# A transformer block on one core: DMA transposes, aligned padded layouts, and MLP blocks paired to 256 tokens

## The chip, the cores and the metric

The kernel runs on one core of one Trainium2 chip. Times are device microseconds (us) of one execution. The metric is the median over several executions. A run counts as "fast" if it is within 1.5% of the fastest run of the same kernel in its batch.

## The reference

One block of a transformer in bf16: S = 2048 tokens, D = 448, 16 heads of 28, MLP width F = 1792. A conditioning vector gives six rows (shift, scale and gate for each half).

```python
mod = (silu(c) @ w_mod)             # six rows: sa, ca, ga, sb, cb, gb
h = layernorm(x) * (1 + ca) + sa
x = x + ga * A(h)                   # attention: 8 keys per query, every second token
h = layernorm(x) * (1 + cb) + sb
x = x + gb * B(h)                   # B: y = layernorm(h); gelu(y @ w1 + b1) @ w2 + b2
return x
```

Because a query sees every second token only, the kernel splits the tokens into two streams of 1024, and a query then sees 8 neighbours of its stream.

## The kernel before

The matmuls of this kernel hold the contracted features on partitions in both operands, while its layernorms leave tokens on partitions, so the kernel transposes the activations in between. This happens twice for each 128-token block: `z` before q/k/v, and `y` before the first MLP matmul. Before the change TensorE does it by multiplying with an identity, four 128x128 pieces into PSUM, and VectorE copies the result to SBUF:

```python
def transpose_tiles(dst_ps, col_slice, src, nrows_src, koff):
    for kt in range(KT):
        nc.tensor.transpose(out=dst_ps[:, kt, col_slice], in_=src[0:nrows_src, koff[kt]:koff[kt] + 128],
                            identity=ident[0:nrows_src, 0:nrows_src])

def front_end_ln(c4):                       # z of four blocks
    ...
    for pair in range(2):
        ptr = ps_small([128, KT, 256], BF16, "ptr")
        ...
            normalize(z[:, 0:D], x_all[:, bs4[i], :], mv, rs, i)
            transpose_tiles(ptr, slice(bi * 128, (bi + 1) * 128), z, 128, KOFF_A)
        nc.vector.tensor_copy(out=hT[:, :, col0:col0 + 256], in_=ptr[:])

def mlp_front(b):                           # y of one block, first MLP matmul, gelu
    pty = ps_small([128, KT, 128], BF16, "pty")
    ...                                     # two layernorms on VectorE, with a pow on GpSimd in each
    normalize(yb[:, 0:D], h2[:], mv2, rs2, 0)
    transpose_tiles(pty, slice(0, 128), yb, 128, KOFF_A)
    nc.vector.tensor_copy(out=yT[:], in_=pty[:])
    for fq in range(0, FT, 8):
        ...     # w1: 128x128 weights, 128 columns of yT; p1 is shared with the logits
        g = nc.scalar.activation(out=hm[:, fq:fq + nf, :], in_=p1[:, 0:nf, :], func=ACT.Gelu_apprx_tanh)

def mlp_back(b, hm):                        # second MLP matmul, residual, store
    for ft in range(FT):
        nc.tensor.matmul(p2[:], lhsT=hm[:, ft, :], rhs=w2_s[:, ft, :], ...)
```

The kernel alternates between groups of attention blocks (exp on ScalarE) and groups of MLP blocks (gelu on ScalarE), so that ScalarE changes its table seldom (the trace has ten table loads of 1.28 us each: five at the gelu, four at the attention's exp, one in the setup). The second MLP matmul of a group is held back and handed out to the attention blocks that follow, one MLP block to each, as filler for TensorE:

```python
phases = [(range(0, 5), [0, 1]), (range(5, 9), [2, 3, 4, 5]), (range(9, 14), [6, 7, 8, 9]),
          (range(14, 16), [10, 11, 12]), (range(16, 18), [13, 14, 15])]
for (gs, mlp_bs) in phases:
    for g in gs:
        attention_block(...)
        if pending_back: mlp_back(*pending_back.pop(0))     # one filler per attention block
        if g in fe_after: front_end_ln(fe_after[g]); front_end_qk(fe_after[g])
    ...
    for b in mlp_bs: mlp_front(b); pending_back.append((b, hm))
```

The order of instructions within each engine's queue is chosen by a scheduler from the data dependencies; the timelines below show the order in which they ran.

The softmax here doesn't subtract the row's maximum and nothing guards it: scores larger than these inputs give would overflow.

## Time and profile before

The median of the first four runs is 267.75 us (266.85 to 269.57). The profiled run is the slowest of these, 269.57 us with a span of 267.6 us.

The busy table and the slices of the profile of the kernel before. A digit is the busy share of one fortieth of the span in tenths; PEclk is the clock that TensorE was granted, in tenths of full speed.

```profile
...
PE 210.6 (79%) x2216; PEld 142.6 (53%) x2220; DVE 157.6 (59%) x360; ACT 103.0 (39%) x136; POOL 69.4 (26%) x107
...
PE   0004895984987797999896999999899889995995
...
PEclk9999997998699999999997999999999999999799
...
```

The groups that the change touches (line, engine, operation, out and in, count; then busy time in us and mean ns of one; then idle time of the engine just before them and what ended it):

```profile
...
L381 PE MATMUL p<-yT,w_s 128*128 128x128 bf16 x896 | 56.0, 225 | 5.7 <-DVE yT L372 5.4 <-ACT hm L385 0.3
...
L372 DVE COPY yT<-pty 128x512 bf16<-128x512 bf16 x16 | 6.5, 415 | 1.5 <-PE pty L165 1.5
...
L165 PE MATMUL ptr<-ident,zbuf 128*128 128x128 bf16 x64 | 6.2, 241 | 24.0 <-DVE zbuf L160 23.6 <-DVE gbb_bc L287 0.3
L165 PE MATMUL pty<-ident,ybuf 128*128 128x128 bf16 x64 | 5.7, 219 | 4.9 <-DVE ybuf L160 2.5 <-DVE ob L396 1.9 <-DVE kT L197 0.5
L183 DVE COPY hT<-ptr 128x1024 bf16<-128x1024 bf16 x8 | 5.3, 677 | 0.1
...
```

The transposes cost 11.9 us of TensorE and their copies 11.8 us of VectorE. That is the busy time that a DMA transpose takes off the two busiest engines.

What TensorE waited for (us in total, number of waits, longest):

```profile
...
PE p L381 <- DVE yT L372: 5.4, 3, 2.7
PE pq L191 <- DVE kT L197: 5.2, 2, 3.7
PE pb_ga L268 <- DMA wmod<-in_w_mod_dram: 2.8, 1, 2.8
PE pty L165 <- DVE ybuf L160: 2.5, 1, 2.5
...
PE pty L165 <- DVE ob L396: 1.9, 1, 1.9
...
```

And the round trip of `y` in the timeline (start, length, engine, instruction, count). Before the matmul at 105.10 there are two transposes on TensorE and one copy on VectorE:

```profile
...
103.87 0.38 PE L165 MATMUL pty<-ident,ybuf 128*128 128x128 bf16 x4
...
104.03 0.68 DVE L197 CAST kT<-pq 128x512 bf16<-128x512 f32 x1
104.63 0.41 DVE L372 COPY yT<-pty 128x512 bf16<-128x512 bf16 x1
104.77 0.38 PE L165 MATMUL pty<-ident,ybuf 128*128 128x128 bf16 x4 [0.52 <-DVE kT L197]
...
105.10 3.29 PE L381 MATMUL p<-yT,w_s 128*128 128x128 bf16 x56
...
```

### The profile page before, as it was taken

What the parts mean: (1) busy time and instruction counts of PE and PEld (TensorE: products, weight loads), DVE (VectorE), ACT (ScalarE), POOL (GpSimd) and SP (SyncE); (2) the same over time, 40 slices, a digit from 0 to 9 for tenths busy, and PEclk for the clock granted to TensorE, in tenths of its full rate; (3) what the DMA queues carried; (4) which work ended last, traced back from release to release, by engine and by line L of the source; (5) the groups of instructions that cost most, each with busy time, mean ns of one, the idle gap of its engine ahead of it and who ended that gap; (6) DMA issues with size and microseconds to landing.
All of it is one profiled execution on the core that took longest, in us unless ns stands there. A gap on an engine that the chain in (4) does not pass through costs nothing.

```text
span 267.6 us, 5246 instructions
## 1 busy us (share of the span) xinstructions
PE 210.6 (79%) x2216; PEld 142.6 (53%) x2220; DVE 157.6 (59%) x360; ACT 103.0 (39%) x136; POOL 69.4 (26%) x107
## 2 busy tenths in 40 slices
PE   0004895984987797999896999999899889995995
PEld 0003332641553555756775866578855488554962
DVE  0199981898386888046888065797526740576101
ACT  0200230870142240874651754455473236722220
POOL 5066150399013132002342001333101300023000
PEclk9999997998699999999997999999999999999799
DMA  7997344000000000000000000000000100000001
GB/s 235 237 327 209 126 114 147 0 2 0 0 0 2 0 0 2 4 17 21 0 2 0 2 20 17 17 20 2 2 0 20 36 20 2 17 17 20 2 16 35
DMA packets 9544, 11.45 MB, mean 43 GB/s; under 512 B 1265, under 2 KB 7729, under 8 KB 9522
## 3 DMA queue, kind: packets, MB, share of 16 engines
q1 hardware_dynamic: 6610, 7.81, 9.7%
q10 hardware_dynamic: 2912, 3.33, 4.0%
q8 instruction: 17, 0.28, 0.4%
q14 instruction: 5, 0.04, 0.1%
HBM read 9.29 MB, written 1.84 MB: 42 GB/s over the span
## 4 chain that ended last, share of the span: by engine, by line
PE 38%; DVE 33%; POOL 9%; DMA 7%; issue 6%; ACT 5%; SPq 1%; POOLq 0%; ACTq 0%
PE p L381 13%; PE p L393 9%; DVE st_ln L151 6%; POOL rs_ln L156 5%; PE po L335 5%; DVE et L330 4%; DMA x_all<-in_A_x_dram 3%; DMA wmod<-in_w_mod_dram 3%; PE pv L309 3%; DVE on L339 2%; DVE ob L396 2%; DVE h L364 2%; ACT et L326 2%; DVE x_all L352 2%; DVE z L160 2%
## 5 line engine op out<-in xcount | busy, mean ns | idle before, releaser
L381 PE MATMUL p<-yT,w_s 128*128 128x128 bf16 x896 | 56.0, 225 | 5.7 <-DVE yT L372 5.4
L381 PEld LDWEIGHTS <-w_s 128*128 128x128 bf16 x896 | 53.9, 101 | 7.4 <-DVE yT L372 4.1
L393 PE MATMUL p<-w_s,hm 128*128 128x448 bf16 x224 | 47.2, 353 | 0.3 <-ACT vbuf L311 0.3
L385 ACT ACTIVATE hm<-p 128x1024 bf16<-128x1024 f32 (+1 forms) x32 | 29.2, 917 | 42.1 <-PE p L381 42.0
L359 POOL TENSOR_TENSOR x1p_ring<-x_all,gbb_bc 128x448 f32<-128x448 bf16 x16 | 18.5, 1154 | 97.8 <-DVE x_all L352 91.5
L156 POOL TENSOR_TENSOR rs_ln<-tv_ln,neg_half 128x1 f32<-128x1 f32 (+1 forms) x36 | 21.4, 600 | 64.6 <-DVE tv_ln L154 53.2
L191 PE MATMUL pq<-hT,Wqk 128*128 128x512 bf16 x124 | 31.5, 397 | 8.2 <-DVE kT L197 5.2
L326 ACT ACTIVATE et<-lt 121x912 bf16<-121x912 f32 x36 | 31.9, 935 | 2.9 <-PE lt L320 2.7
L330 DVE TENSOR_TENSOR et<-et,mask_rest 121x1824 bf16<-121x1824 bf16 x18 | 22.0, 1228 | 15.9 <-ACT et L326 15.8
L393 PEld LDWEIGHTS <-hm 128*128 128x128 bf16 x224 | 20.6, 98 | 17.0 <-issue 0.3
L396 DVE TENSOR_TENSOR ob<-p,x1p_ring 128x448 bf16<-128x448 f32 x16 | 9.8, 614 | 33.1 <-PE p L393 33.1
L191 PEld LDWEIGHTS <-Wqk 128*128 128x128 bf16 x128 | 12.7, 101 | 24.3 <-issue 12.0
L151 DVE BATCH_NORM_STATS2 st_ln<-x_all 128x6 f32<-128x448 bf16 x32 | 18.9, 611 | 11.2 <-DMA x_all<-in_A_x_dram 11.2
L165 PE MATMUL ptr<-ident,zbuf 128*128 128x128 bf16 x64 | 6.2, 241 | 24.0 <-DVE zbuf L160 23.6
L311 ACT CAST vbuf<-pv 121x448 bf16<-121x448 f32 x18 | 9.6, 535 | 30.4 <-PE pv L309 30.3
L335 PEld LDWEIGHTS <-et 121*114 121x114 bf16 x288 | 17.2, 132 | 5.2 <-DVE et L330 4.0
L299 POOL TENSOR_TENSOR w_s<-w_s,gb_bc 128x448 bf16<-128x448 bf16 x14 | 16.6, 1221 | 12.0 <-ACT gb_bc L286 12.0
L335 PE MATMUL po<-vbuf,et 121*114 121x29 bf16 x288 | 17.8, 202 | 2.1 <-DVE et L330 2.1
L309 PE MATMUL pv<-Wv,hT 128*121 128x448 bf16 x72 | 18.0, 370 | 0.7 <-DVE kT L197 0.7
L343 ACT COPY oT<-pt 128x456 bf16<-128x456 bf16 (+1 forms) x18 | 9.7, 540 | 22.4 <-PE pt L165 22.4
L165 PEld LDWEIGHTS <-zbuf 128*128 128x128 bf16 x64 | 4.4, 107 | 25.0 <-DVE zbuf L160 24.5
L350 PE MATMUL pw<-wo_s,oT 128*128 128x448 bf16 x64 | 14.9, 355 | 1.5 <-ACT oT L343 1.2
(76 smaller groups left out, 237.7 us busy)
## 6 DMA issues: line engine op xcount, KB each, us to landing
x_all<-in_A_x_dram SPq DMA_DIRECT2D x16, 112.0 KB, 5.2
out_dram<-ob SPq DMA_DIRECT2D x16, 112.0 KB, 1.7
w_s<-in_B_w_dram ACTq DMA_DIRECT2D x1, 1568.0 KB
w_s<-in_B_w_dram SPq DMA_DIRECT2D x1, 1344.0 KB, 7.0
wmod<-in_w_mod_dram SPq DMA_DIRECT2D x1, 1344.0 KB, 8.5
wqkv_st<-in_A_wqkv_dram ACTq DMA_DIRECT2D x1, 1008.0 KB, 8.4
wmod<-in_w_mod_dram SPq DMA_DIRECT2D x1, 768.0 KB, 7.7
wo_s<-in_A_wo_dram ACTq DMA_DIRECT2D x1, 336.0 KB, 8.5
```

Of the source, the lines that this page charges most:

```text
L151: nc.vector.bn_stats(out=st[:], in_=src)
L156: nc.gpsimd.tensor_tensor(out=rs[:], in0=tv[:], in1=neg_half[:, 0:n], op=ALU.pow)
L191: nc.tensor.matmul(pq[:], lhsT=Wqk[:, kt, m, :], rhs=hT[:, kt, cc0:cc0 + 512], start=(kt == 0), stop=(kt == KT - 1))
L299: nc.gpsimd.tensor_tensor(out=w2_s[:, ft, :], in0=w2_s[:, ft, :], in1=gb_bc[:], op=ALU.mult)
L309: nc.tensor.matmul(pv[0:BK, :], lhsT=hT[:, kt, k0:k0 + BK], rhs=Wv[:, kt, :], start=(kt == 0), stop=(kt == KT - 1))
L326: ex = nc.scalar.activation(out=et_v[:, 2 * half:2 * half + 2], in_=lt[0:BK, :, 0:4 * BQ].rearrange("p r (ft c) -> p r ft c", ft=4), func= ...
L330: nc.vector.tensor_tensor(out=et[0:BK], in0=et[0:BK], in1=mask_rest[0:BK], op=ALU.mult)
L335: nc.tensor.matmul(po[0:BQ, h, :], lhsT=et[0:BK, h, :], rhs=vb[0:BK, h, :], start=True, stop=True)
L359: nc.gpsimd.tensor_tensor(out=x1p_ring[:, b % NX1P, :], in0=x1_blk(b), in1=gbb2_bc[:], op=ALU.add)
L381: mm = nc.tensor.matmul(p1[:, f, :], lhsT=w1_s[:, kt, ft * 128:(ft + 1) * 128], rhs=yT[:, kt, :], start=(kt == 0), stop=(kt == KT - 1))
L385: g = nc.scalar.activation(out=hm[:, fq:fq + nf, :], in_=p1[:, 0:nf, :], func=ACT.Gelu_apprx_tanh)
L393: nc.tensor.matmul(p2[:], lhsT=hm[:, ft, :], rhs=w2_s[:, ft, :], start=(ft == 0), stop=(ft == FT - 1))
```

## The change

The intent is to take both transposes off TensorE and VectorE, by `dma_start_transpose` on SyncE's queue; to lay out the padded buffers for these transfers (512 columns, a pad of 16, the constant-one row at partition 64 of the last k tile; ScalarE now writes the bias row in place, and a detour by DMA, 1.8 us to landing in the trace before, goes away); to load `x` in four transfers, not 16, and store four blocks at a time; and to process MLP blocks in pairs, so that the first MLP multiplies 256 columns per loaded weight. The core of the diff:

```diff
-    zbufs = [cst.tile([128, D + 1], BF16, ...
+    zbufs = [cst.tile([128, DP], BF16, ...          # DP = 512; ybufs likewise
 ...
-        for pair in range(2):
-            ptr = ps_small([128, KT, 256], BF16, "ptr")
-            ...
-                transpose_tiles(ptr, slice(bi * 128, (bi + 1) * 128), z, 128, KOFF_A)
-            nc.vector.tensor_copy(out=hT[:, :, col0:col0 + 256], in_=ptr[:])
+        for i, b in enumerate(bs4):
+            normalize(z[:, 0:D], x_all[:, b, :], mv, rs, i)
+            nc.sync.dma_start_transpose(out=hT[:, :, tok_col(b):tok_col(b) + 128], in_=z[:])
 ...
-        nc.scalar.copy(out=brow[96:128, ch * D:(ch + 1) * D], in_=pb[96:128, :])
-    nc.sync.dma_start(out=Wqk[127:128, ...], in_=brow[127:128, 0:2 * D]...)
-    nc.sync.dma_start(out=Wv[127:128, KT - 1, :], in_=brow[127:128, 2 * D:3 * D])
+        if ch < 2: nc.scalar.copy(out=Wqk[KA:KA + 1, KT - 1, 4 * ch:4 * ch + 4, :]..., in_=pb[KA:KA + 1, :]...)
+        else:      nc.scalar.copy(out=Wv[KA:KA + 1, KT - 1, :], in_=pb[KA:KA + 1, :])
 ...
-    def mlp_front(b):
-        yT = big.tile([128, KT, 128], BF16, name="yT", tag="yT")
-        transpose_tiles(pty, slice(0, 128), yb, 128, KOFF_A)
-        nc.vector.tensor_copy(out=yT[:], in_=pty[:])
+    def mlp_front(j):
+        yT = big.tile([128, KT, 256], BF16, name="yT", tag="yT")
+        for bi, b in enumerate([2 * j, 2 * j + 1]):
+            ...
+            nc.sync.dma_start_transpose(out=yT[:, :, bi * 128:(bi + 1) * 128], in_=yb[:])
 ...
-    def mlp_back(b, hm):
+    def mlp_back(j, hm):
+        for bi in range(2):                           # both blocks of the pair in one call
 ...
-        (range(0, 5), [0, 1]), (range(5, 9), [2, 3, 4, 5]), (range(9, 14), [6, 7, 8, 9]),
-        (range(14, 16), [10, 11, 12]), (range(16, 18), [13, 14, 15]),
+        (range(0, 5), [0]), (range(5, 9), [1, 2]), (range(9, 14), [3, 4]),      # pairs
+        (range(14, 16), [5]), (range(16, 18), [6, 7]),
```

Some clearing of buffers also moves from GpSimd to VectorE.

## The prediction

> **What bounds the kernel now.** The page's busy table gives TensorE 210.6 us (79% of 267.6), VectorE 157.6, ScalarE 103.0, GpSimd 69.4. So no engine is full; the kernel is TensorE work plus about 57 us in which TensorE waits. Windows by stage: 0–33 us setup, TensorE busy 8.2 us; 33–50 setup, 13.3 of 17; 50–105 attention with the q/k front end, TensorE 44.2 and VectorE 42.6 of 55; from 105 on TensorE is busy 90% with MLP work, except 116–143 (22.9 of 27), 197–215 (15.4 of 18) and 230–248 (13.6 of 18), where it waits for layernorm chains. The chain of waits mixes TensorE (38%) and VectorE (33%): both matter.
>
> **What the change removes** (groups view, timeline):
> - 128 TensorE transposes of z and y: 6.2 + 5.7 = 11.9 us of TensorE.
> - VectorE copies of their results: hT 5.3, yT 6.5 = 11.8 us.
> - 896 first-MLP matmuls of 128 columns become 448 of 256. The timeline shows 58.7 ns apiece (56 in 3.29 us), 52.6 us in all; the 448-column second-MLP matmuls pace about 200 ns (11 in 2.25 us). Estimate for 256 columns from these: 110 ns, so 49 us: a gain of only 3–4 us.
> - The bias row's trip by DMA (brow). Its copies leave at 31.75 and 33.24 and land 1.8 us later; only then does the wmod2 load leave (35.1), and TensorE waits for it until 43.7. Written in place by ScalarE, the load can leave at about 32.7: about 2.4 us saved, on the path.
>
> **What it adds.** 32 DMA transposes of 128x512 on SP's queue. No transpose is in this trace. Estimate: the small on-chip copy lands in 1.8 us; [...] against about 1.3 us for TensorE transpose plus copy (first ybuf to yT). [...] The final store holds four blocks instead of one (landing 1.7 us today): estimate +1.5 us. A pair's matmuls wait for both blocks.
>
> **Regrouping.** The last two phases go from 3+3 blocks to 2+4. At 240–248 TensorE now waits for blocks 14 and 15 (1.6 + 2.5 us idle, then a cold clock: 112 matmuls in 8.05 instead of 6.25 us). Pair 12/13 will be ready there and fills the gap: 3–4 us.
>
> **Sum.** TensorE −15.5, setup −2.4, tail −3.5; against it [...] store +1.5; VectorE relief helps in 50–105 but overlaps the TensorE saving. Net about −14 us. I predict 254 us, 80% range 245 to 265; faster by over 2% 0.73, within 2% 0.16, slower 0.11.
>
> **What would show each step right.** TensorE busy near 195; VectorE near 146; wmod2 landing near 41; first-MLP matmuls pacing 105–115 ns; [...] TensorE idle unchanged or smaller in 50–105 and the tail; w1 waits on DMA yT of at most 2 us per phase.
>
> **What would make it wrong.** Transposes that land in over 5 us or occupy SP for several us each: 32 in one queue then hold up z (three buffers) and both blocks of a pair, and TensorE idles. Early z transposes queue behind the weight loads (DMA 70–90% busy until 27 us). [...]

What no trace of this case shows is cut from it, and the cuts are marked: how long a DMA transpose takes to issue and to land, with the latency that followed from it, and two of the risks. The sum came to about −14 us with latency in it, as a cost. Its term is cut, so the terms that still stand (−15.5, −2.4, −3.5 and +1.5) come to −19.9 and not to −14. The "cold clock" is in the trace of the kernel before: the granted clock is 1.00 from 236 to 248 us, and 0.50 for 3.41 us from 248.55.

## More of the kernel before

`ps_small` is a ring of PSUM slots that the transposes share with the q/k, v and second-MLP results.

No fast run of the kernel before was profiled.

No engine is full. TensorE is busy 79% of the span and has 57 us of waiting; VectorE is next with 59%.

The same run by stage, from the windows view (columns: stretch, its length, each engine's busy time and instruction count, TensorE clock, DMA share, GB/s). The first stretch ends when the matmul of the attention gate (`pb_ga`) starts, the second with the last q/k matmul.

```profile
...
0.00:43.70 43.70, 15.53 (x92) 7.54 (x93) 26.83 (x66) 5.31 (x9) 17.07 (x45) 1.00 0.71 213
43.70:103.90 60.20, 49.65 (x373) 26.90 (x377) 44.47 (x84) 21.53 (x34) 24.50 (x25) 0.91 0.00 1
103.90:267.60 163.70, 145.46 (x1753) 108.14 (x1751) 86.25 (x211) 76.19 (x93) 27.81 (x37) 0.98 0.04 13
...
```

In the setup the DMA engines are 71% busy and TensorE does little. In the middle stage TensorE is busy 49.7 of 60.2 us, at a mean clock of 0.91. The MLP stage has 145.5 of 163.7 us.

At 104.77 TensorE had stood idle for 0.52 us, and the trace puts this down not to data but to `kT L197`, the cast of a q/k result that ends at 104.71: by the source the transpose needs a slot of the PSUM ring that the q/k results use too. The copy of the transposed `y` itself ran on VectorE after that same cast.

## The result, and the profile after

The kernel after takes 244.07 us (median of 11 runs, 242.39 to 245.67). The kernel before, on the same chip, takes 267.18 us (median of 16, 260.16 to 271.36). All runs of the kernel after are fast ones. Of the kernel before only three of 16 are (260.16, 261.61 and 263.66); the others lie between 265 and 271. The ratio is 0.9318 (95% interval 0.9259 to 0.9376). It is the mean time of one kernel's fast runs over that of the other's of the same rounds, so it is not quite the ratio of the medians, which is 244.07 / 267.18 = 0.9135. The result's own label says "unclear", but the interval lies wholly below 0.98, and no run of either kernel overlaps one of the other. So the gain is some 18 us against the fast runs of the kernel before, and 23 us against its typical run.

The profiled run of the kernel after took 243.73 us, span 242.0 us. The busy table of its page:

```profile
...
PE 199.8 (83%) x1637; PEld 126.8 (52%) x1644; DVE 147.7 (61%) x349; ACT 101.4 (42%) x136; POOL 67.7 (28%) x102
...
```

The windows of its three stages, cut at the same two events as before:

```profile
...
0.00:40.40 40.40, 14.74 (x76) 7.05 (x78) 25.31 (x75) 5.40 (x9) 16.93 (x40) 0.96 0.91 250
40.40:86.70 46.30, 43.19 (x331) 22.63 (x336) 35.86 (x70) 21.02 (x34) 23.06 (x23) 1.00 0.16 32
86.70:242.00 155.30, 141.85 (x1235) 97.10 (x1232) 86.50 (x205) 75.01 (x93) 27.71 (x40) 0.96 0.10 25
...
```

The setup is 3.3 us shorter, the middle stage 13.9 us, the MLP stage 8.4 us. TensorE's work shrank by 10.8 us and its waiting by 14.8 us (57.0 to 42.2). A part of the middle stage's difference may belong to the slow run that was profiled of before (clock 0.91 against 1.00), so the stages must not be read as a decomposition. The experiments give one.

Its group of the first MLP, with half the instructions and twice the columns:

```profile
...
L380 PE MATMUL p<-yT,w_s 128*128 128x256 bf16 x448 | 55.6, 280 | 3.4 <-DMA yT<-ybuf 2.1 <-ACT et L323 0.9 <-ACT hm L384 0.4
...
```

The DMA view of the kernel after, for the transposes (number, median us from issue to landing):

```profile
...
hT<-zbuf SPq DMA_TRANSPOSE x16, 2.9
yT<-ybuf SPq DMA_TRANSPOSE x16, 2.4
...
```

In the trace one occupies SyncE's queue for 1.2 us in the median (at most 2.1). The slowest `hT` landing takes 7.8 us; that transpose is issued at 32.01 us, beside the second modulation load (from 29.25 us, 9.2 us to landing). The early ones run beside the weight loads too: the DMA share in the windows view is 1.12 from 16 to 24 us and 1.04 from 30 to 39 us.

TensorE's wait of 5.4 us for `yT` has shrunk to 2.1 us, and the wait for the modulation load is gone from its list of waits:

```profile
...
PE p L380 <- DMA yT<-ybuf: 2.1, 1, 2.1
...
```

### The profile page after: what moved, and what is told of

Same layout as the page of the kernel before. It is cut to its first block, busy times and chain, and to the rows that moved or that the text cites. A ratio compares the mean times of both kernels' runs of the same rounds, so it can differ in the third digit from the quotient of the medians.

```text
span 242.0 us, 4113 instructions
## 1 busy us (share of the span) xinstructions
PE 199.8 (83%) x1637; PEld 126.8 (52%) x1644; DVE 147.7 (61%) x349; ACT 101.4 (42%) x136; POOL 67.7 (28%) x102
## 3 DMA queue, kind: packets, MB, share of 16 engines
q1 hardware_dynamic: 23554, 11.89, 19.9%
## 4 chain that ended last, share of the span: by engine, by line
PE 55%; DVE 21%; POOL 6%; DMA 6%; ACT 6%; issue 4%; SPq 1%; POOLq 0%; ACTq 0%; DVEq 0%
PE p L380 13%; PE p L393 13%; PE pq L183 8%; PE po L332 6%; PE pw L349 5%; DVE st_ln L151 4%; POOL rs_ln L156 4%; DMA x_all<-in_A_x_dram 4%; DVE et L327 3%; PE pv L306 3%; ACT hm L384 3%; PE lt L317 2%; DVE x_all L351 2%; PE pbias L230 2%; POOL x1p_ring L359 2%
## 5 line engine op out<-in xcount | busy, mean ns | idle before, releaser
L380 PE MATMUL p<-yT,w_s 128*128 128x256 bf16 x448 | 55.6, 280 | 3.4 <-DMA yT<-ybuf 2.1
L380 PEld LDWEIGHTS <-w_s 128*128 128x128 bf16 x448 | 44.2, 101 | 12.1 <-issue 4.5
L393 PE MATMUL p<-w_s,hm 128*128 128x448 bf16 x224 | 45.7, 353 | 0.0
L359 POOL TENSOR_TENSOR x1p_ring<-x_all,gbb_bc 128x448 f32<-128x448 bf16 x16 | 16.7, 1043 | 70.5 <-DVE x_all L351 65.4
L395 DVE TENSOR_TENSOR x_all<-p,x1p_ring 128x448 bf16<-128x448 f32 x16 | 9.9, 620 | 26.8 <-PE p L393 26.8
L306 PE MATMUL pv<-Wv,hT 128*121 128x448 bf16 x72 | 20.1, 383 | 0.0
L206 PE MATMUL ps_col<-silu_bf,wmod 128*128 128x1 bf16 (+1 forms) x32 | 1.5, 174 | 21.9 <-DVE silu_bf L198 21.9
L296 POOL TENSOR_TENSOR w_s<-w_s,gb_bc 128x448 bf16<-128x448 bf16 x14 | 15.8, 1166 | 9.0 <-ACT gb_bc L283 9.0
L317 PEld LDWEIGHTS <-kT 28*121 28x121 bf16 x288 | 11.1, 137 | 11.1 <-issue 10.9
L351 DVE TENSOR_TENSOR x_all<-pw,x_all 128x448 bf16<-128x448 f32 x16 | 9.9, 620 | 10.3 <-PE pw L349 10.3
L317 PE MATMUL lt<-qT,kT 28*121 28x114 bf16 x288 | 14.9, 235 | 1.0 <-ACT et L323 0.5
```

What stands on the lines that cost most here:

```text
L306: nc.tensor.matmul(pv[0:BK, :], lhsT=hT[:, kt, k0:k0 + BK], rhs=Wv[:, kt, :], start=(kt == 0), stop=(kt == KT - 1))
L317: mm = nc.tensor.matmul(lt[0:BK, rr, ft * BQ:(ft + 1) * BQ], lhsT=kT[32 * r:32 * r + DH, ft, k0:k0 + BK], rhs=qT[32 * r:32 * r + DH, ft, q ...
L359: nc.gpsimd.tensor_tensor(out=x1p_ring[:, b % NX1P, :], in0=x1_blk(b), in1=gbb2_bc[:], op=ALU.add)
L380: mm = nc.tensor.matmul(p1[:, f, :], lhsT=w1_s[:, kt, ft * 128:(ft + 1) * 128], rhs=yT[:, kt, :], start=(kt == 0), stop=(kt == KT - 1))
L393: nc.tensor.matmul(p2[:], lhsT=hm[:, ft, bi * 128:(bi + 1) * 128], rhs=w2_s[:, ft, :], start=(ft == 0), stop=(ft == FT - 1))
```

## The experiments

Twelve kernels ran, in three batches of four, each batch on one chip beside runs of the kernel before. The medians of the kernel before are 266.85, 266.35 and 267.61 us in the three batches, so kernels of different batches can be compared to about half a per cent. All gave the right result, and every profile shown of them is of a fast run. Each was timed four times. One run of z_on_tensor (250.65 us) and one of y_on_tensor_unpaired (260.74 us) are slow ones; without them the medians are 246.64 and 256.21 us. The ratios to before that are given below come from the third batch, in which no run of the kernel before was under 266.04 us, so that all of them count as fast there; they can't be set beside the 0.9318 above, whose fast runs of before are those of 260 to 264 us. The differences in us are the safer measure. I name them by what they are:

| kernel | z transposed by | y transposed by | MLP blocks | median us (range) |
|---|---|---|---|---|
| before | TensorE | TensorE | 128 | 267.18 (260.16 to 271.36) |
| after | DMA | DMA | 256 | 244.07 (242.39 to 245.67) |
| z_on_tensor | TensorE | DMA | 256 | 248.2 (246.48 to 250.65) |
| y_on_tensor | DMA | TensorE | 256 | 261.54 (260.88 to 262.56) |
| no_dma_transpose | TensorE | TensorE | 256 | 266.89 (266.62 to 269.58) |
| unpaired | DMA | DMA | 128 | 239.16 (238.85 to 241.36) |
| layout_only | TensorE | TensorE | 128 | 261.81 (260.58 to 262.08) |
| y_on_tensor_unpaired | DMA | TensorE | 128 | 256.44 (254.78 to 260.74) |

My first theory, before any experiment, was that the `z` transposes bring most of the gain (10 to 14 us), since the middle stage, where `z` is made, had shrunk most. Its rivals: that `y`'s transposes bring it; and that the layout and the merged loads bring it, with transposes worth only their busy time. A letter in a quoted expectation stands for the theory whose numbers that expectation gives. Two half sentences on an in-order queue of TensorE, which no trace shows as such, are cut from the expectations and marked.

### One part back at a time: z_on_tensor, y_on_tensor, no_dma_transpose, layout_only

Edits to the kernel after, for `z` and for `y`; no_dma_transpose has both, and layout_only both and blocks of 128:

```diff
# z
-            nc.sync.dma_start_transpose(out=hT[:, :, tok_col(b):tok_col(b) + 128], in_=z[:])
+            pe_transpose(ptr, slice(bi * 128, (bi + 1) * 128), z)          # four per block
+        nc.vector.tensor_copy(out=hT[:, :, col0:col0 + 256], in_=ptr[:])  # per two blocks
# y
-            nc.sync.dma_start_transpose(out=yT[:, :, bi * 128:(bi + 1) * 128], in_=yb[:])
+            pty = ps_small([128, KT, 128], BF16, "pty")
+            pe_transpose(pty, slice(0, 128), yb)
+            nc.vector.tensor_copy(out=yT[:, :, bi * 128:(bi + 1) * 128], in_=pty[:])
```

> The kernel after, with only the front end's z transposes put back on TensorE (64 transposes into the two-slot PSUM ring, 8 hT copies on VectorE); y stays on DMA, pairs stay. Theory A (the gain sits in the q/k front-end stage[...]): 10 to 14 us slower than after, nearly all of it between the modulation matmuls and the last q/k matmul, with TensorE waits on VectorE back and the clock dipping. Theory B (only the engine time counts: 6.2 us of TensorE, 5.3 us of VectorE): 4 to 7 us slower.

> The kernel after, with only the MLP's y transposes put back on TensorE (64 transposes, 16 yT copies of 128x512 on VectorE). Theory A and B alike: TensorE gets 5.7 us back, but it waits for layernorm chains there anyway and the chain gets about 1 us shorter per pair: 2 to 6 us slower than after, none of it in the front-end stage beyond 1 us.

(On the "about 1 us": the traces show a landing of 2.4 us in the kernel after against 1.2 us in the kernel before, from the transpose at 103.87 us to the end of the copy at 105.04.)

> The kernel after with both transposes on TensorE: what is left is the padded layout, the in-place bias row, the merged loads and stores and the pairing. Theory A: 14 to 18 us slower than after, so 5 to 9 us faster than before. Theory B: 9 to 12 us slower than after, so 12 to 15 faster than before.

> Neither DMA transposes nor pairs: padded layout, bias row in place, merged loads and stores, blocks of 128 tokens in the phases of before. If the first four runs add up (DMA for z worth 5 us, for y 17, pairing costs 5): 239 + 22 = 261 to 263 us, so 4 to 6 us under before, of it 3 to 4 us before the modulation matmuls. If the layout alone is worth nothing: 266 to 268.

Putting `z` back costs 4.1 us by the medians (248.2 against 244.07), 2.6 us by the fast runs alone (246.64), and 5.4 us with `y` already back (266.89 against 261.54). Putting `y` back costs 17.5 us (261.54), where I had expected 2 to 6, and both together 22.8 us, more than either theory allowed. My first theory fell. With `z` back, the middle stage does grow by 9 us (46.3 to 55.2), but the setup is 2.2 us shorter and the MLP stage shorter too, so most of it is given back.

layout_only takes 261.81 us. That is 5 us less than the typical run of the kernel before, but no less than its fast ones (259.75 and 260.04 us in this batch). So how much the layout brings depends on which runs of before one compares with: 5 us or nothing. Part of the 13.9 us of the middle stage is therefore not the transposes' doing: layout_only's middle stage is already 54.1 us, at a clock of 0.97.

### No pairs: unpaired

```diff
-        bs = [2 * j, 2 * j + 1]
+        bs = [j]                    # yT, hm and p1 for 128 tokens, NHM 6, phases as before the change
```

> The kernel after with the MLP blocks of 128 tokens again and the phases of before (3+3 blocks at the end), DMA transposes kept. Both theories: the first-MLP matmuls go back to about 58 ns apiece (3 us more), and the last phase again waits for blocks 14 and 15 (3 us more): 4 to 8 us slower than after, nothing before the first MLP matmul. If pairing is worth nothing: within 1 us.

Without pairs the kernel is *faster*: 239.16 us, 4.9 us under the kernel after. The three kernels layout_only, unpaired and after, all with little scatter, give the decomposition: DMA transposes −22.65 us (261.81 to 239.16), pairing with its regrouping +4.91 us (239.16 to 244.07). Their sum, −17.7 us, is the whole gain over the fast runs of before (mean 261.8). Pairs cost the same where TensorE transposes: +5.1 us from layout_only to no_dma_transpose, and +5.1 us from y_on_tensor_unpaired to y_on_tensor.

TensorE's clock is what differs. The MLP stage of unpaired:

```profile
...
86.70:237.00 150.30, 136.92 (x1676) 100.45 (x1673) 85.62 (x206) 75.99 (x93) 29.40 (x40) 1.00 0.11 26
...
```

The stage is 5.0 us shorter than the one of the kernel after, of which 4.9 us are TensorE busy time, at a clock of 1.00 against 0.96. In the MLP stage of the kernel after the granted clock is 1.0 but for three stretches of 0.5, each of 3.41 us, which begin at 107.76, 152.13 and 223.81 us (a fourth begins at 240.88, after TensorE's last matmul). Half clock for three times 3.41 us costs 5.1 us by my estimate, which is about the 4.9 us. Here is the first of them, in windows from 106 us (TensorE's busy time, then the clock):

```profile
...
106.00:108.00 2.00, 1.30 (x25) 0.94 0.00 0
108.00:110.00 2.00, 2.00 (x21) 0.50 0.03 8
110.00:112.00 2.00, 2.00 (x15) 0.71 0.00 0
...
```

And TensorE's timeline of the kernel after around it:

```profile
...
94.43 4.71 PE L393 MATMUL p<-w_s,hm 128*128 128x448 bf16 x24
...
103.25 0.97 PE L306 MATMUL pv<-Wv,hT 128*121 128x448 bf16 x4
...
106.88 1.01 PE L332 MATMUL po<-vbuf,et 121*114 121x29 bf16 x16 [0.70 <-DVE et L327]
...
108.44 1.75 PE L306 MATMUL pv<-Wv,hT 128*121 128x448 bf16 x4
...
```

At 94.43 both blocks' second MLP (24 matmuls seen here and four more at 99.85, of 28) runs in one go, because `mlp_back` of a pair is handed to a single attention block. The later attention blocks of the phase then have no filler. TensorE has a gap of 0.70 us before 106.88, and from 108 to 110 the granted clock is 0.50: four v matmuls take 1.75 us where the same four took 0.97 at 103.25. In the MLP stage of this trace the granted clock is 1.0 or 0.5 and nothing between, with 3.41 us to each fall. From 94 us on no gap before this fall is longer than 0.70 us, and only that one is over 0.5 us. Nor does the length of a pause decide. In unpaired TensorE waits 2.65 us for a DMA transpose until 217.24, and keeps its clock:

```profile
...
213.70:217.20 3.50, 0.88 (x16) 1.00 0.18 37
217.20:220.70 3.50, 3.30 (x56) 1.00 0.15 31
...
```

It was busy 0.88 of 3.5 us there, and the kernel after 2.74 of the 3.5 us from 104.20. The first two falls come where the second MLP has run out (its last matmuls before them end at 100.77 and 146.30 us) and only attention's matmuls are left; the third follows a wait of 2.05 us for a DMA transpose. So the trace shows where the time went. What makes the clock fall, the pauses or the kind of matmul that fills the stretch, isn't shown.

### The lump taken apart: pair_split_back

If the lump is the cause, and not the width of 256, then a kernel that keeps the pairs in the first MLP but hands out the second MLP block by block must be at least as fast as unpaired.

```diff
-    def mlp_back(j, hm):
-        for bi in range(2):
+    def mlp_back(j, hm, bi):
-            pending_back.append((j, hm))
+            pending_back += [(j, hm, 0), (j, hm, 1)]
```

> The kernel after (244 us), still with pairs of 256 tokens in the first MLP, but the second MLP is handed out one block at a time to the attention blocks, as in the unpaired kernels. If pairing costs its 5 to 6 us through the second MLP going out in one lump (TensorE starves in the later attention blocks and its clock falls to 0.73 to 0.79): 238 to 240 us, granted clock near 0.99. If the wide matmul or the wait for both blocks costs it: 242 to 244.

(The 0.73 to 0.79 are the mean granted clocks of two windows of the kernel after, 0.79 from 106 to 109 us and 0.73 from 109 to 113.)

It takes 236.91 us (235.83 to 237.44), ratio to before 0.8858 (0.8809 to 0.8908). That is 7.2 us under the kernel after, by an edit of a few lines, and 2.3 us under unpaired. The window of its MLP stage:

```profile
...
86.70:234.10 147.40, 136.35 (x1238) 94.83 (x1236) 85.52 (x207) 75.14 (x93) 29.91 (x40) 1.00 0.11 26
...
```

The second MLP in the same part of its timeline:

```profile
...
95.18 2.82 PE L393 MATMUL p<-w_s,hm 128*128 128x448 bf16 x14
...
100.60 1.30 PE L393 MATMUL p<-w_s,hm 128*128 128x448 bf16 x6
...
```

The second MLP now comes as 14, 1, 6, 4 and 3 matmuls between attention pieces (two of the groups are shown), and the clock stays at 1.00. The stage is 7.9 us shorter than that of the kernel after: 5.5 us of TensorE's busy time and 2.4 us of its waiting. That is not the luck of one profile: the mean clock is 0.982 to 0.993 in the four runs of this kernel and 0.979 to 0.992 in those of unpaired, against 0.964 to 0.977 in the twelve of the kernel after. So the lump cost 7 us, and the wide matmul, with the regrouping, is worth some 2 us (the ranges of the two do not overlap, but they ran on different chips). Of the 2.9 us by which the stage is shorter than that of unpaired only 0.6 us is TensorE's busy time, so most of it isn't the arithmetic saving that the prediction had in mind.

### Is it the work of y's transposes, or the way they sit in the chain? extra_transposes, extra_transposes_and_copies, y_on_tensor_unpaired

The largest item is `y`: y_on_tensor_unpaired, which differs from unpaired only in how `y` is transposed, takes 256.44 us against 239.16. But 64 transposes are 5.7 us of TensorE and 16 copies 6.5 us of VectorE. Two theories: either the work on two busy engines costs this much, or the place of the work does: the first MLP can't start until a transpose has had its turn in TensorE's queue and a copy its turn in VectorE's. To tell them apart, unpaired gets the same work, but nobody waits for it: the first MLP reads what the DMA transposed, and the TensorE transposes (and, in the second variant, the copies) go to scratch.

```diff
             nc.sync.dma_start_transpose(out=yT[:, :, bi * 128:(bi + 1) * 128], in_=yb[:])
+            pty = ps_small([128, KT, 128], BF16, "pty")
+            pe_transpose(pty, slice(0, 128), yb)
+            yT2 = big.tile([128, KT, 128], BF16, name="yT2", tag="yT2")   # second variant only
+            nc.vector.tensor_copy(out=yT2[:], in_=pty[:])                  # second variant only
```

> The unpaired kernel with DMA transposes, plus the 64 TensorE transposes of y into the same two-slot PSUM ring, results read by nobody (no VectorE copy; the first MLP still waits for the DMA). If the cost of y on TensorE is TensorE's own time [...]: 7 to 13 us slower than unpaired, 246 to 252. If it is the round trip (transpose, VectorE copy, first MLP) and the copies: at most 6 us slower, 241 to 245.

> The unpaired kernel (239.2 us) with y back on TensorE and VectorE (z stays on DMA). The paired kernels put y at 17 us; unpaired, z and y together are 22.7 us. If the parts add up: 239 + 17 = 254 to 257 us. If y costs only what the extra transposes cost: 243 to 244.

> The unpaired kernel with the same TensorE transposes and VectorE copies as the run beside it, but the copies go to a scratch tile and the first MLP still reads the DMA's result. If the work itself costs the time (TensorE 5.7 us, VectorE 6.5 us): equal to the run beside it, 252 to 257 us. If the round trip does (the first MLP waits for a transpose in TensorE's queue and a copy in VectorE's queue): 244 to 248 us.

Measured: extra_transposes 243.5 us (241.86 to 244.77), extra_transposes_and_copies 243.79 us (242.96 to 244.4; ratio to before 0.9107, interval 0.9059 to 0.9154), y_on_tensor_unpaired 256.44 us (ratio 0.9561, interval 0.9501 to 0.962). So the work costs 4.6 us (243.79 less 239.16); nearly all of that is TensorE's, and the copies are about free. The remaining 12.7 us (256.44 less 243.79; 12.4 by the fast runs alone) come from the dependency. The last two kernels do the same work; their MLP stages in the windows view, first of y_on_tensor_unpaired:

```profile
...
88.40:254.30 165.90, 145.72 (x1752) 108.40 (x1751) 90.06 (x222) 76.19 (x93) 29.55 (x40) 0.97 0.04 13
...
```

And of extra_transposes_and_copies:

```profile
...
88.90:242.60 153.70, 141.00 (x1739) 104.53 (x1738) 89.13 (x221) 75.97 (x93) 28.29 (x40) 1.00 0.10 26
...
```

The stage is 12.2 us longer with the dependency: TensorE idles 20.2 us in it against 12.7, and is busy 4.7 us longer for the same instructions, at a clock of 0.97 against 1.00. The timelines show what happens to the first `y`. In y_on_tensor_unpaired:

```profile
...
74.47 0.40 DVE L160 TENSOR_SCALAR ybuf<-h,mv_ln,rs_ln 128x448 bf16<-128x448 bf16 x1 [0.51 <-POOL rs_ln L156]
...
88.60 0.38 PE L171 MATMUL pty<-ident,ybuf 128*128 128x128 bf16 x4 [0.21 <-DVE kT L194]
...
89.84 0.41 DVE L378 COPY yT<-pty 128x512 bf16<-128x512 bf16 x1
...
90.30 0.89 PE L387 MATMUL p<-yT,w_s 128*128 128x128 bf16 x13
...
```

In unpaired:

```profile
...
72.64 0.40 DVE L160 TENSOR_SCALAR ybuf<-h,mv_ln,rs_ln 128x448 bf16<-128x448 bf16 x1 [0.51 <-POOL rs_ln L156]
...
73.10 1.19 SPq L371 DMA_TRANSPOSE yT<-ybuf  x1
...
77.59 0.33 PE L380 MATMUL p<-yT,w_s 128*128 128x128 bf16 x3
...
```

In the first, `y` is written from 74.47, but its transpose runs at 88.60: TensorE runs the q/k matmuls first (the last wait before the transpose, 0.21 us, is for a `kT`), and VectorE the casts of their results before the copy, at 89.84. The first MLP starts at 90.30, 15.8 us after `y`. In the second the DMA takes `y` at 73.10, and the first MLP's matmuls are at hand from 77.59, 5.0 us after `y`, as filler between q/k and attention. extra_transposes_and_copies has them at 79.74.

This first block is an extreme one. Reckoned in the same way for all sixteen blocks, from the start of the normalization to the first matmul that reads the result, the mean is 18.0 us in y_on_tensor_unpaired and 14.7 us in each of unpaired and extra_transposes_and_copies; most of it is time in which TensorE has other work. Nor is the cost paid at the first block: against extra_transposes_and_copies, y_on_tensor_unpaired has its fifth `y` 2.2 us later, the ninth 6.4 us, the thirteenth 7.9 us, and its end 11.7 us. The delay builds up from phase to phase.

TensorE's waits agree in part: in y_on_tensor_unpaired 5.4 us for the copy of `yT` and 5.6 us in the transposes' own waits (2.5, 1.9 and 1.2; two of the three are shown), one kind of them again for `kT`; in extra_transposes_and_copies 2.3 us for the DMA. In unpaired the wait for the DMA is 4.8 us, so what is surely gone are the transposes' own waits. The lines of y_on_tensor_unpaired:

```profile
...
PE p L387 <- DVE yT L378: 5.4, 3, 2.7
...
PE pty L171 <- DVE ybuf L160: 2.5, 1, 2.5
...
PE pty L171 <- DVE kT L194: 1.2, 2, 1.0
...
```

What this does not settle: the scheduler orders each queue around the dependencies, so the order in the queue, the shared PSUM ring and the wait itself changed together. No run has the transposes in another PSUM ring.

### The last phases: unpaired_2_4

The prediction counted 3 to 4 us for regrouping the last two MLP phases from 3+3 to 2+4 blocks. Alone, on unpaired:

```diff
-        (range(14, 16), [10, 11, 12]), (range(16, 18), [13, 14, 15]),
+        (range(14, 16), [10, 11]), (range(16, 18), [12, 13, 14, 15]),
```

> The unpaired kernel (239.2 us) with only the grouping of the pairs: last two phases 2+4 blocks instead of 3+3. If the 5 us that pairing costs come from the grouping of phases: 242 to 244 us. If they come from the pair as a unit (both blocks' second-MLP matmuls issued in one go, so later attention blocks have no filler and TensorE's clock drops): 238 to 240 us with a granted clock near 0.99 after 87 us. The prediction's step, 2+4 being worth 3 to 4 us, would give 235 to 236.

It takes 238.1 us (237.21 to 239.38) against 239.16 (238.85 to 241.36), on another chip. The ranges overlap. It is worth 1 us at most, if anything.

### The setup: mask_early_z8 and best_setup_2_4

In the kernel after GpSimd is idle from 4.5 to 14.9 us, and then builds the attention mask just when VectorE makes the first `z`. In the timeline of the kernel after:

```profile
...
16.01 4.12 DVE L160 TENSOR_SCALAR zbuf<-x_all,mv_ln,rs_ln 128x448 bf16<-128x448 bf16 x3 [0.49 <-POOL rs_ln L156]
...
19.93 1.87 POOL L252 TENSOR_SCALAR_AFFINE_SELECT mask_rest<-mask_rest 128x1824 bf16<-128x1824 bf16 x1
...
20.05 1.77 DVE L198 TENSOR_TENSOR silu_bf<-e_c,c_col 128x4 bf16<-128x4 f32 x1
...
27.54 0.37 DVE L160 TENSOR_SCALAR zbuf<-x_all,mv_ln,rs_ln 128x448 bf16<-128x448 bf16 x1
...
```

Three normalizations take 4.12 us, where a single one later takes 0.37, and the tiny product that makes `silu_bf` takes 1.77 us; the matmuls that compute the shift and scale rows wait for it until 21.87 us. The slow stretch lies beside GpSimd's work on the mask: the 128x4 product ends at 21.82 us, and the mask instruction beside it at 21.80. By what means the one would hold up the other isn't shown; that the mask does it was my estimate. I moved the mask ahead, to where GpSimd is idle, and gave `z` eight buffers:

```diff
-    nc.gpsimd.memset(mask_rest[:], 1.0)            # and both affine_selects: from after the q/k front end ...
+    nc.gpsimd.memset(mask_rest[:], 1.0)            # ... to right after the identity is built
-    NZB = 3
+    NZB = 8
```

> The unpaired kernel with two edits in setup: the attention mask is built at the start on GpSimd, which waits from 4.5 to 15 us, instead of beside VectorE's z normalizations (4.1 us for three that take 0.4 each elsewhere), and eight z buffers instead of three (the fourth z ran at 27.5 us, 7.5 after the third, and the first q/k matmul waited for it until 31.6). Expected: bias-row matmuls at 19 to 21 instead of 24, first q/k matmul at 27 to 29, 234 to 236 us. If the weight loads bound setup: no change, 239.

On unpaired this gives 234.8 us (234.65 to 235.86), 4.4 us less (on another chip), the fastest kernel and faster than both kernels that were compared. In its trace `silu_bf` takes 0.15 us:

```profile
...
15.40 0.15 DVE L203 TENSOR_TENSOR silu_bf<-e_c,c_col 128x4 bf16<-128x4 f32 x1
...
```

(It runs there beside GpSimd's power instruction of 128x4 elements, 14.91 to 15.93 us by the rough records of that engine, and takes 0.15 us all the same.) Its bias matmuls start at 17.48 us, not 24.04, and `pb_ga` at 36.98, not 40.41. Which share the eight buffers have was not tried alone.

The last run was to add the 2+4 phases and to move the other clearing on GpSimd ahead as well:

```diff
-    nc.gpsimd.memset(Wqk[64:128, KT - 1, :, :], 0.0)   # and of Wv, wo_s, vbufs, ybufs, w1_s:
+    nc.gpsimd.memset(Wqk[64:128, KT - 1, :, :], 0.0)   # all to right after the identity is built
```

> The run with the early mask and eight z buffers (234.8 us), plus the 2+4 grouping (worth 1.1 us unpaired) and the other GpSimd memsets moved to the start too (silu and z ran at two to three times their usual time beside them). Expected 232 to 234 us; if the weight loads bound setup, 233.7.

(The "two to three times" are from the trace of mask_early_z8, where GpSimd clears buffers from 16.00 to 21.82 us: the copy of silu to all columns takes 1.22 us at 16.00, against 0.42 in the kernel before, and four `z` take 3.22 us at 18.74, against 1.31 at 29.33.)

It takes 236.06 us (235.61 to 237.95; ratio to before 0.8833, interval 0.878 to 0.8887), which is no gain: a miss. In its trace the first q/k matmul starts at 33.37 us, later than in mask_early_z8 (27.51), because the scheduler put the first four `z` behind all scaling of the weights on VectorE: they start at 23.67 us, not 18.74. An emptier GpSimd queue changed the order elsewhere. A kernel with the split pairs and the early mask together was not run.

## Why the prediction was right or wrong

The direction was right: faster by over 2%, to which I gave 0.73. The size came out larger than predicted. I said 254 us with a range of 245 to 265. The ratio of fast runs times 267.75 is 249.5 us, inside the range; the measured median of 244.07 us is 0.9 us below its low end. I gave −14; it was −18 against the fast runs of before and −23 against its typical run. That the total came so near is in part luck, as two large errors went opposite ways. The steps:

- **The latency of the DMA transposes, counted as a cost: wrong in sign, and the step that failed.** I took the 1.3 us between the first `ybuf` and `yT` as the price of the old way, a longer one, an estimate that no trace showed, as that of the new, and charged the difference to every exposed chain. The landing is longer (2.4 us measured for `y`). But here a chain of two engines' queues took longer than its instructions. In the kernels that differ in nothing else, the first `y` waited 15.8 us for its first matmul by way of TensorE and VectorE, and 5.0 us by way of the DMA (means over all blocks 18.0 and 14.7). Instead of costing time, the longer but independent path gained about 12.7 us for `y` alone. The 2.5, 1.9 and 5.4 us waits in the trace before and the timeline at 104 us were there to be read, and I did not.
- **"TensorE −15.5": about right in the trace, too large as a gain.** Without pairs TensorE's busy time is 194.6 us (I said near 195); after, it is 199.8, at a lower clock (0.969 against 0.992). But the transposes of `y` cost only 4.3 us of the time when nothing waits for them, and `z`'s, with their dependency, 2.6 to 5.4 us.
- **"VectorE near 146"**: 147.7. Right, and worth about nothing by itself: adding the 16 copies back moved the time by 0.3 us.
- **Wide matmuls, "a gain of only 3–4 us"**: 110 ns was a fair estimate (26 of them in 3.00 us at a clock of 1.00 is 115 ns). As done, pairing *cost* 4.9 us, which I had not foreseen: I read the pair as an arithmetic saving, and did not ask what its second half does to the filler of the attention blocks. With the second MLP handed out block by block it gains 2.3 us, regrouping included.
- **Regrouping, "3–4 us"**: 1.1 us by medians, not told apart from zero. The gap at the end that it was to fill is still there in the kernel after: TensorE waits 2.05 us for a `yT` until 223.54, and the 56 matmuls that follow take 7.94 us, with a clock of 0.50 from 223.81 to 227.22, where 56 take 6.27 us in pair_split_back.
- **Setup, "about 2.4 us saved"**: `pb_ga` starts 3.4 us earlier (43.73 to 40.36), and the second modulation load leaves at 29.25 us, not 35.07. Right in mechanism.
- **Store "+1.5"**: landing 3.3 us against 1.7. Right.
- **What would make it wrong**: transposes landing late beside the weight loads did occur (7.8 us the slowest) and cost little. TensorE's clock fell to 0.50 three times in the MLP stage: two of the falls stand where the lump left no filler, and the third after a wait of 2.05 us for a DMA transpose.

Two steps failed in opposite directions: the sign of the latency (forecast as a cost, measured as −12.7 us) and the pairing (about 12 us from −7, with the regrouping, to +5). They work against each other in the sum, which is why the total was closer than its parts.

What stays open: which of queue order, PSUM ring and wait makes `y`'s round trip long; what makes TensorE's clock fall; why the kernel before takes 260 us in some runs and 266 to 271 in most; and so whether the layout is worth nothing or 5 us.

## What to carry to other kernels

Judge a transpose by the queues that it passes, not by its length: the one that needed a turn on TensorE and then one on VectorE came late here (15.8 us from the first `y` to its first matmul), while a DMA that takes longer by itself (2.4 us against 1.2) but passes neither left the next matmuls free to be filler (5.0 us). When work is batched, look at what it was filling before: handing out the second MLP in lumps of two starved later attention blocks, went with a clock of 0.50 on TensorE in two stretches of 3.41 us, and turned a gain of 2 us into a loss of 5. And before believing a stage-by-stage difference of two traces, put back one part at a time; the stage that shrank most was not the one whose change mattered most.
